# Eight token tiles turned in 32x32 blocks on VectorE and through DRAM, in place of TensorE transposes

## The chip, the cores and the metric

The kernel runs on one core of a Trainium2 chip. The metric is the time of one execution in device microseconds (us). The runs shown of the kernel before are 1119.29, 1119.57 and 1120.29 us; their median is 1119.57.

## The reference

The computation is one transformer-like block on x of 2048 tokens and 576 channels, in float32, where two branches work on the same normalised tokens:

```
xn  = (x - mean(x)) / sqrt(var(x) + 1e-5)            # over the 576 channels of each token
A   = attention(xn @ wqkv) @ wo                      # 32 heads of 18; each token looks at 8 keys,
                                                     # its own and those 2, 4, ... 14 tokens back
B   = mish(xn @ w1 + b1) @ w2                        # 576 -> 4608 -> 576
out = x + A + B
```

## The kernel before

The tokens are worked through in two halves of 1024 (`hf` 0 and 1), each half in two blocks of 512 tokens (`b`), each block in four tiles of 128 tokens (`jj`). A half runs through four stages: its tiles are normalised and transposed, the q, k and v products are made in groups of heads (`qkv_item`, L327), the feed-forward branch runs in 18 steps of `m1_part` (first product, Mish) and `m2_pair` or `m2_cols` (second product), and beside the feed-forward steps GpSimd and VectorE work on the attention. The output projection of both halves comes last.

A float32 operand is split into a high part, rounded to the type that TensorE multiplies, and a low part, the rest; three products (high x high, high x low, low x high) make one. So every tile of tokens has to be turned, with channels as rows, and split: `transpose_split` (L67) does it. TensorE turns four 128x128 pieces into one PSUM bank (L75), the last 64 channels into a second bank (L76), and for the second block the rests `rem` of the tile of the first block as well (L78). ScalarE rounds both banks into the high part in SBUF (L81, L86), VectorE subtracts that from the banks for the low part (L82, L87). Ahead of it ScalarE normalises the tile in place (`norm1`, L139) and GpSimd copies its last 64 channels once more beside them (L140), so that high and low of these channels share one matmul; GpSimd also keeps or subtracts `rem` (L192, L194).

The order of the work is written out by hand. A list `plan` holds the items of TensorE in order: `q` for a q, k and v product, `m` and `p` for the parts of a feed-forward step, `t` for a tile that is turned, `z` and `o` for others. `before(i, fn)` hangs other work onto item i: loads, casts, normalisation. When the program is built, the list is walked once and every engine gets its instructions in that order and keeps it. All DMAs are issued from SyncE's one queue (SP), in that order too; a DMA that waits holds up those behind it. The DMAs use eight semaphores in turn, so a DMA also waits until the one eight before it has landed.

Tiles in SBUF and PSUM come from pools with a fixed number of buffers per tag, used in turn; a new tile waits until the last user of the one before in its buffer is done. Those that matter here: `xn` (5 buffers: tokens and scratch), `raw` (4 buffers: weights as loaded), and in PSUM `h` and `out` (4 banks each). The matmuls of `m2_pair` (L759) write into `out` banks, which VectorE adds to the accumulators (L763), and the turned pieces of the second half's first three tiles take two `out` banks each. The matmuls of `m1_part` (L661, L667) and of `qkv_item` (L348) write into `h` banks; the Mish of a step reads one of them (L707), and an add on VectorE (L706) precedes the Mish of others.

The change lies where the first half ends and the second begins. The eight tiles of the second half are loaded (`x_load`, L103), normalised and turned (`tr`, L1222) while TensorE does the last three feed-forward steps of the first half and, for the second block, the first q, k and v products of the second half. The items around it are, in order: the step q = 17 with the second products of step 16 between its parts, and three turned tiles between those; the fourth turned tile; the second products of step 17, with q items of the second half between them; and a turned tile ahead of or behind each of the next q items.

Of the kernel before, what the change touches and what calls it, by code (L numbers as in the profile page):

```python
# [8 lines left out]
F32 = mybir.dt.float32  # L9
# [5 lines left out]
S, D, F = 2048, 576, 4608  # L15
H, DH, W, DIL = 32, 18, 8, 2
HALO = (W - 1) * DIL
P = 128
# [4 lines left out]
TJ = SH // P  # L23
JB = TJ // NB
KT = D // P
NF = F // P
NP = NF // 2
# [12 lines left out]
def block_kernel(ctx: ExitStack, tc: tile.TileContext, x, wq, wo, w1, b1, w2, mask, out):  # L40
    nc = tc.nc
    tpn = iter(range(1000))

    const = ctx.enter_context(tc.tile_pool(name="const", bufs=1))
    sb = ctx.enter_context(tc.tile_pool(name="sb", bufs=2))
    ps = ctx.enter_context(tc.tile_pool(name="ps", bufs=4, space=bass.MemoryType.PSUM))
    dram = ctx.enter_context(tc.tile_pool(name="dram", bufs=1, space=bass.MemoryType.DRAM))
# [13 lines left out]
    ident = const.tile([P, P], F32, name="ident")  # L61
# [2 lines left out]
    for k in range(30):  # L64
        nc.tensor.transpose(warm[:, (k % 4) * P:(k % 4 + 1) * P], ident, ident)

    def transpose_split(src, dst, col, extra=None, pair=False):  # L67
        n = next(tpn)
        if pair:
            ta, tb = (ps.tile([P, 512], F32, tag="out", bufs=4, name=f"tt{k}_{n}") for k in range(2))  # L70
        else:
            ta = ps.tile([P, 512], F32, tag="h", bufs=4, name=f"ta_{n}")
            tb = ps.tile([P, 512], F32, tag="h", bufs=4, name=f"tb_{n}")
        for k in range(KT):
            nc.tensor.transpose(ta[:, k * P:(k + 1) * P], src[:, k * P:(k + 1) * P], ident)  # L75
        nc.tensor.transpose(tb[:, 0:P], src[:, KT * P:(KT + 1) * P], ident)  # L76
        if extra is not None:
            nc.tensor.transpose(tb[:, P:2 * P], extra, ident)  # L78
        tav = ta.rearrange("p (k t) -> p k t", k=KT)
        hi = dst[:, 0:KT, col:col + P]  # L80
        nc.scalar.copy(hi, tav)  # L81
        nc.vector.tensor_sub(dst[:, 5:5 + KT, col:col + P], tav, hi.bitcast(F32))  # L82
        e = 1 if extra is None else 2
        hr = dst[:, KT:KT + 5 * e - 4:5, col:col + P]
        tbv = tb.rearrange("p (k t) -> p k t", k=KT)[:, 0:e]
        nc.scalar.copy(hr, tbv)  # L86
        nc.vector.tensor_sub(hr[64:P], tbv[64:P], hr[64:P].bitcast(F32))  # L87

    XTs = {}
    rems = {}  # L90
    xns = {}
    XNB = 5
# [7 lines left out]
    def x_tile(hf, n):  # L100
        return x[hf * SH:(hf + 1) * SH, :].rearrange("(p j) d -> p j d", j=TJ)[:, n, :]

    def x_load(n):  # L103
        xn = sb.tile([P, 5 * P], F32, tag="xn", bufs=XNB, name=f"xn_1_{n}_{next(tpn)}")
        nc.sync.dma_start(xn[:, 0:D], x_tile(1, n))
        xns[1, n] = xn

# [29 lines left out]
    def norm1(n):  # L137
        xn = xns[1, n]
        nc.scalar.activation(xn[:, 0:D], xn[:, 0:D], AF.Identity, bias=nm1[:, n, :], scale=rs1[:, n, :])  # L139
        nc.gpsimd.tensor_copy(xn[:, D:D + 64], xn[:, KT * P:D])  # L140

    group = {}

    def ln_group(ns):
# [39 lines left out]
    def ln_transpose(hf, b, jj):  # L184
        if jj == 0:
            XTs[hf, b] = sb.tile([P, 9 + b, TB], F32R, tag=f"xt{b}", bufs=1, name=f"xt_{hf}_{b}")
        xn = xns[hf, b * JB + jj]
        if (b, jj) == (0, 0):
            rems[hf] = sb.tile([P, JB, P], F32, tag="tt", bufs=2, name=f"rem_{hf}")
        rem = rems[hf][:, jj, :]  # L190
        if b == 0:
            nc.gpsimd.tensor_copy(rem, xn[:, KT * P:])  # L192
        else:
            nc.gpsimd.tensor_tensor(out=rem, in0=rem, in1=xn[:, KT * P:], op=ALU.subtract)  # L194
        transpose_split(xn, XTs[hf, b], jj * P, rem if b else None, (hf, b) == (1, 0) and jj < 3)

    def raw_load(src, width, name):
        raw = sb.tile([P, 5 * P], F32, tag="raw", bufs=4, name=f"r{name}")
# [176 lines left out]
    BUFS = {"wb": 3, "wc": 2, "wa0": 1, "a0": 3, "a1": 2, "acc": 9, "raw": 4, "tt": 2, "r3": 1, "mn": 5, "xn": XNB}  # L375
# [764 lines left out]
    at = {}  # L1140
# [7 lines left out]
    def before(i, fn):  # L1148
        plan[max(i, 0)][1].append(fn)
# [188 lines left out]
    def spot(hf, q, i):  # L1338
        return at["s", hf, q, i]

    for q in range(NP):
        if q == 0:
            i = at["q", 0, 3, 1, 0]
            ps_ = dict(raw=i - 3, sums=i - 1, wa=i, wc=i + 1, t0=i + 2, t1=i + 4)
        elif q == 1:
            i = at["q", 0, 3, 0, 0]
# [16 lines left out]
    for q in range(1, 2 * OC + 1):  # L1363
        i = spot(0, q, (3,2)[q > 1])
# [5 lines left out]
    i = spot(0, NP - 1, 0)  # L1370
# [5 lines left out]
    i = at["q", 1, 0, 1, 1]  # L1376
# [4 lines left out]
    i = spot(0, 9, 4)  # L1381
    for k in range(2):
        for n, steps in enumerate((
# [33 lines left out]
    for n, (a, b) in enumerate((("P6", "P1"), ("P7", "P6"), ("P6", "P5"), ("P2", "P1"), ("P3", "P6"), ("P4", "P7"), ("P5", "P7"))):  # L1417
        for pr in range(2):
            i = items[-2][2] + 1 + (0,1,2)[n] if n < 3 else at["p", 1, J + 0 - 1, n > 4, pr] + (1, 7, 1, 2)[n - 3]
# [6 lines left out]
    i = at["q", 0, 1, 1, 0]  # L1426
# [3 lines left out]
    i = at["q", 0, 3, 1, 0]  # L1430
# [5 lines left out]
    i = at["q", 1, 0, 1, 1]  # L1436
    for n in range(8):
        c, k = divmod(n, 4)
        d = i + (0, 1, 3, 4, 6, 8, 10, 12)[n]
        before(d, lambda c=c, k=k: s_step(1, c, k))  # L1440
        d = max(d + 2, (at["q", 1, 1, 1, 2], at[("z", 1, 2)])[c] if k == 3 else 0)
# [4 lines left out]
    for n in range(0, JB, 2):  # L1446
        i = at["q", 0, 1, 0, n]
# [4 lines left out]
    for n in range(TJ):  # L1452
        i = spot(0, 2 + n, 2)
        before(i, lambda n=n: x_load(n))
        before(i + 5, lambda n=n: stats1(n))
    before(i + 6, var1)
    i = spot(0, NP - 2, 0)
    for jj in range(JB):
        before(i + 2 * jj, lambda jj=jj: x_load(jj))
        before(i + 2 * jj + 6, lambda jj=jj: norm1(jj))  # L1460
        before(at["t", 1, 0, jj] + 2, lambda jj=jj: x_load(JB + jj))
    for jj in range(JB):
        before(at["p", 0, NP - 1, 1, 1] + jj, lambda jj=jj: norm1(JB + jj))

    for n, (name, pr) in enumerate((name, pr) for name in ("P4", "P5", "P2", "P3") for pr in range(2)):
        i = items[dict(P4=0, P5=2, P3=2, P2=3)[name]][2] + pr
# [122 lines left out]
```

## Time and profile before

| what | value |
|---|---|
| median of the runs | 1119.57 us |
| span of the profiled execution | 1118.2 us |
| what lies around the span, by that median | 1.4 us |
| TensorE busy | 1109.2 us, 99% |
| VectorE busy | 835.2 us, 75% |
| GpSimd busy | 777.4 us, 70% |
| ScalarE busy | 491.7 us, 44% |
| time taken by DMA packets, share of 16 engines | 69.8% on SP's queue |
| granted clock of TensorE | 1.00 |

The profiled execution has no time of its own beside its span; the time that lies around it is taken as the difference to the median of the runs. In the profile PE is TensorE, PEld its weight loads, DVE is VectorE, ACT ScalarE, POOL GpSimd and SPq the queue of SyncE from which the DMAs are issued. A line such as `L75` is a line of the kernel before. A row of the timeline gives the start in us, the duration, the engine, the line, the operation with output and inputs, the count, and in brackets how long the engine sat idle before it and what released it. A row of the DMA issues gives output and input, the count, the size of each and the median time from issue to landing.

### The profile page before, as it was taken

The numbers are of one execution on the slowest core, as the hardware profiler recorded it, in microseconds if no ns is written. First come the engines' busy times: TensorE is split into PE (matmuls) and PEld (weight loads), VectorE is DVE, ScalarE is ACT, GpSimd is POOL, SyncE is SP. The second block draws the span as 40 slices with busy tenths as digits, with TensorE's granted clock in tenths as the row PEclk, the third lists the DMA queues.
The fourth block names the chain that finished last, engine by engine and source line by source line (L and its number), as shares of the span: only waits on it lengthen the run. The fifth ranks groups of instructions, "written<-read, shape, count | busy, mean of one in ns | idle before, by whom it ended". The sixth has DMA issues, their size and how long they took to land.

```text
span 1118.2 us, 18402 instructions
## 1 busy us (share of the span) xinstructions
PE 1109.2 (99%) x6630; PEld 1023.9 (92%) x6630; DVE 835.2 (75%) x1355; ACT 491.7 (44%) x892; POOL 777.4 (70%) x631
## 2 busy tenths in 40 slices
PE   8999999999999999999999999999999999999998
PEld 8999899999999999999999888989999999999998
DVE  6369788888888888887656566687866677776876
ACT  5544645544554545555233354343433343443332
POOL 2479777767689687685787346666789878668632
PEclk9999999999999999999999999999999999999999
DMA  6899695868767849666696797665655477576463
GB/s 200 284 311 313 227 357 205 294 227 282 260 241 265 273 169 342 226 240 215 208 332 234 240 378 254 225 200 188 220 192 190 173 266 270 207 258 243 160 217 108
DMA packets 147487, 271.08 MB, mean 242 GB/s; under 512 B 30114, under 2 KB 86724, under 8 KB 147396
## 3 DMA queue, kind: packets, MB, share of 16 engines
q1 hardware_dynamic: 147396, 269.91, 69.8%
q8 instruction: 52, 0.85, 0.3%
q14 instruction: 39, 0.32, 0.1%
HBM read 160.39 MB, written 109.48 MB: 241 GB/s over the span
## 4 chain that ended last, share of the span: by engine, by line
PE 94%; DVE 3%; POOL 1%; ACT 1%; issue 1%; DMA 0%; SPq 0%; DVEq 0%; POOLq 0%; ACTq 0%
PE h L661 30%; PE po L759 20%; PE pq L348 11%; PE po L872 10%; PE po L851 7%; PE h L667 6%; PE o L1060 4%; PE z L446 4%; POOL accP L860 1%; DVE accP L875 0%; POOL act L713 0%; DMA acc<-in_x 0%; PE ta L75 0%; DVE og L582 0%; POOL act L814 0%
## 5 line engine op out<-in xcount | busy, mean ns | idle before, releaser
L759 PEld LDWEIGHTS po<-w,act 128*128 128x128 f32 x1728 | 236.4, 188 | 6.0 <-POOL act L713 0.4
L759 PE MATMUL po<-w,act 128*128 128x288 f32 x1728 | 240.7, 295 | 0.1
L576 POOL TENSOR_TENSOR pv<-L,kv 128x576 f32<-128x576 f32 x128 | 176.3, 1477 | 38.5 <-DVE L L569 28.9
L713 POOL TENSOR_TENSOR act<-c,act 128x512 fp32r<-128x512 f32 x81 | 107.6, 1329 | 126.1 <-ACT act L712 124.4
L538 POOL TENSOR_TENSOR pr<-q,kv 128x576 f32<-128x576 f32 x120 | 184.2, 1564 | 7.7 <-DMA q<-q_d 6.0
L763 DVE TENSOR_TENSOR acc<-po,acc 128x288 f32<-128x288 f32 x288 | 120.0, 449 | 31.8 <-PE po L759 30.5
L348 PE MATMUL pq<-wq,xt 128*128 128x432 f32 x672 | 136.4, 361 | 1.2 <-ACT xt L81 1.2
L872 PEld LDWEIGHTS po<-w,act 128*128 128x128 f32 x960 | 131.1, 188 | 3.7 <-DVE accP L875 0.4
L872 PE MATMUL po<-w,act 128*128 128x288 f32 x960 | 133.8, 295 | 0.2
L348 PEld LDWEIGHTS pq<-wq,xt 128*128 128x128 f32 x672 | 125.0, 188 | 8.2 <-ACT xt L81 2.1
L707 ACT ACTIVATE c<-c,b1c 128x512 f32<-128x512 f32 x81 | 58.7, 725 | 130.6 <-DVE c L706 130.2
L661 PE MATMUL h<-S,t 128*128 128x512 f32 x432 | 110.4, 391 | 0.0
L661 PE MATMUL h<-xt,t 128*128 128x512 f32 x432 | 110.4, 391 | 0.0
L695 ACT COPY c<-h 128x512 f32<-128x512 f32 x81 | 47.5, 586 | 133.2 <-PE h L667 75.2
L582 DVE TENSOR_REDUCE og<-pv 128x144 f32<-128x1152 f32 x64 | 85.9, 1343 | 26.8 <-POOL pv L576 26.7
L661 PE MATMUL h<-xt,wa 128*128 128x512 f32 x432 | 104.1, 390 | 0.0
L543 DVE TENSOR_REDUCE L<-pr 128x64 f32<-128x1152 f32 x64 | 85.8, 1342 | 17.6 <-POOL pr L538 17.4
L875 DVE TENSOR_TENSOR accP<-po,accP 128x288 f32<-128x288 f32 x160 | 69.7, 454 | 38.9 <-PE po L872 37.4
L661 PEld LDWEIGHTS h<-xt,wa 128*128 128x128 f32 x432 | 80.9, 188 | 17.0
L851 PEld LDWEIGHTS po<-pw,u 128*128 128x128 f32 x672 | 92.2, 188 | 2.9 <-DVE u L805 0.7
L851 PE MATMUL po<-pw,u 128*128 128x288 f32 x672 | 93.7, 295 | 0.4 <-DVE u L805 0.4
L661 PEld LDWEIGHTS h<-xt,t 128*128 128x128 f32 x432 | 79.1, 188 | 14.7 <-DVE rt L706 0.2
(232 smaller groups left out, 1848.7 us busy)
## 6 DMA issues: line engine op xcount, KB each, us to landing
kv<-kv_d SPq DMA_DIRECT2D x64, 396.0 KB, 5.6
kept_t<-t SPq DMA_DIRECT2D x36, 512.0 KB, 5.2
t<-kept_t SPq DMA_DIRECT2D x36, 512.0 KB, 5.0
rw<-in_w SPq DMA_DIRECT2D x36, 320.0 KB, 4.5
kept_wa<-wa SPq DMA_DIRECT2D x18, 640.0 KB, 4.7
kept_w<-w SPq DMA_DIRECT2D x20, 576.0 KB, 4.1
wa<-kept_wa SPq DMA_DIRECT2D x18, 640.0 KB, 6.3
w<-kept_w SPq DMA_DIRECT2D x20, 576.0 KB, 4.7
```

What stands on the lines that cost most here:

```text
L348: nc.tensor.matmul(pq[:, 0:432], XT[:, xi, tok], wt[wi][:, hl, 0:432], start=i == 0, stop=i == len(seq) - 1)
L538: nc.gpsimd.tensor_tensor(out=pr[:, x:x + hh], in0=q[:, j0 + x:j0 + x + hh, None, :].to_broadcast([P, hh, W, CU]), in1=win(kt, 0, CU, j0 + ...
L543: nc.vector.tensor_reduce(L[:, k, j0:j0 + hj].rearrange("p j w h -> p (j w h)"), pr.rearrange("p j w (h d) -> p (j w h) d", h=2), axis=AX, ...
L576: nc.gpsimd.tensor_tensor(out=pr[:, x:x + hj].rearrange("p j d w -> p j w d"), in0=L[:, k, x:x + hj, :, h:h + 1].to_broadcast([P, hj, W, DH]),
L582: nc.vector.tensor_reduce(og[:, :, c0:c0 + DH], pr, axis=AX, op=ALU.add)
L661: nc.tensor.matmul(ph, wt[:, wl, wk * P:(wk + 1) * P], X[:, xs, :], start=first and i == 0, stop=last and i == len(seq) - 1, skip_group_ch ...
L713: nc.gpsimd.tensor_tensor(out=a[:, 1, :], in0=t, in1=a[:, 0, :].bitcast(F32), op=ALU.subtract)
L759: nc.tensor.matmul(po, acts[hf, q, b, j][:, al, tok], done["w2", hf, 2 * q + j][:, wl, c * HC:(c + 1) * HC], start=i == 0, stop=i == 5)
L763: nc.vector.tensor_tensor(out=t, in0=po, in1=t, op=ALU.add)
L851: nc.tensor.matmul(po, units[e, k, qq][:, al, tok], w[:, qq, wl, :], start=i == 0, stop=i == 5)
L872: nc.tensor.matmul(po, acts[hf, q, b, j][:, al, tok], done["w2", hf, 2 * q + j][:, wl, c * HC:(c + 1) * HC], start=i == 0, stop=i == 5)
L875: nc.vector.tensor_tensor(out=t, in0=po, in1=t, op=ALU.add)
```

## The change

TensorE no longer turns the eight tiles of the second half. Instead:

- VectorE transposes a tile's 32x32 blocks (`x_turn`): within each block of 32 tokens and 32 channels rows and columns change places. The result goes into one SBUF buffer (tag `oT`, one buffer).
- Four DMAs write it, 32 partitions each, to a DRAM tensor of 576 channels by 128 tokens; each moves 576 pieces of 32 elements (128 bytes). Three DMAs read it back (`x_back`) into an `xn` buffer with channels as rows: 512 channels as four pieces side by side, and the last 64 twice, one below the other.
- `transpose_split` copies the read tile with ScalarE into the PSUM banks where TensorE put its result, and the split goes on as before. The second block's `rem` is copied in the same way.
- GpSimd's copy of the last 64 channels in `norm1` is gone, as the double read takes its place.
- Loads, normalisation, turning and reading back have new places in the list. The loads of the second block go to `raw` buffers.

In the order of each engine the change gives the following. TensorE has 44 transposes fewer and is otherwise in the same order. On VectorE the block transposes of the first block stand in step 16: the first behind the first four accumulates (L763) of the second products of step 15, the others behind the later groups of four (the second with one subtraction between). Those of the second block stand behind the split of the second tile, behind the next four accumulates, behind the split of the third tile, and behind the first four accumulates of step 17. On SP, the last tiles' writes and reads stand among the loads of `kv`, `q` and `wq`, some of which come behind them.

```
-    def transpose_split(src, dst, col, extra=None, pair=False):
+    def transpose_split(src, dst, col, extra=None, pair=False, turned=False):
         n = next(tpn)
+        turn = (lambda o, i: nc.scalar.copy(o, i)) if turned else (lambda o, i: nc.tensor.transpose(o, i, ident))
...
-        for k in range(KT):
-            nc.tensor.transpose(ta[:, k * P:(k + 1) * P], src[:, k * P:(k + 1) * P], ident)
-        nc.tensor.transpose(tb[:, 0:P], src[:, KT * P:(KT + 1) * P], ident)
+        if turned:
+            turn(ta, src[:, 0:KT * P])
+        else:
+            for k in range(KT):
+                turn(ta[:, k * P:(k + 1) * P], src[:, k * P:(k + 1) * P])
+        turn(tb[:, 0:P], src[:, KT * P:(KT + 1) * P])
         if extra is not None:
-            nc.tensor.transpose(tb[:, P:2 * P], extra, ident)
+            turn(tb[:, P:2 * P], extra)
...
-        nc.gpsimd.tensor_copy(xn[:, D:D + 64], xn[:, KT * P:D])
-
+
+    def x_turn(n):
+        t = sb.tile([P, D], F32, tag="oT", bufs=1, name=f"xT_{n}")
+        nc.vector.transpose(t, xns[1, n][:, 0:D])
+        d = xT_d[n] = dram.tile([D, P], F32, name=f"xT_d{n}")
+        rows = d.rearrange("(n i) p -> i n p", i=32)
+        for g in range(4):
+            part = slice(g * 32, (g + 1) * 32)
+            nc.sync.dma_start(rows[:, :, part], t[part].rearrange("i (n k) -> i n k", k=32))
+
+    def x_back(n):
+        xn = xns[1, n] = sb.tile([P, 5 * P], F32, tag="xn", bufs=XNB, name=f"xn_t_{n}")
+        nc.sync.dma_start(xn[:, 0:KT * P].rearrange("p (k t) -> p k t", k=KT),
+                          xT_d[n][0:KT * P].rearrange("(k p) t -> p k t", p=P))
+        for r_ in range(2):
+            nc.sync.dma_start(xn[r_ * 64:(r_ + 1) * 64, KT * P:], xT_d[n][KT * P:D])
...
-    i = spot(0, NP - 2, 0)
-    for jj in range(JB):
-        before(i + 2 * jj, lambda jj=jj: x_load(jj))
-        before(i + 2 * jj + 6, lambda jj=jj: norm1(jj))
-        before(at["t", 1, 0, jj] + 2, lambda jj=jj: x_load(JB + jj))
-    for jj in range(JB):
-        before(at["p", 0, NP - 1, 1, 1] + jj, lambda jj=jj: norm1(JB + jj))
+    i, e = spot(0, NP - 3, 8), at["t", 1, 0, JB - 1]
+    for n in range(TJ):
+        b_, jj = divmod(n, JB)
+        turn = e - 4 + 2 * jj if b_ else i + 2 * jj + 5
+        load_at = spot(0, NP - 1, 0) + (1, 2, 4, 6)[jj] if b_ else i + 2 * jj
+        back = e + (1, 2, 4, 7)[jj] if b_ else turn + 4
+        before(load_at, lambda n=n: x_load(n, "raw" if n >= JB else "xn"))
+        before(turn - 1, lambda n=n: norm1(n))
+        before(turn, lambda n=n: x_turn(n))
+        before(back, lambda n=n: x_back(n))
```

More of the change, by code (lines that the diff above doesn't have):

```diff
@@ L101, in x_tile, with x_load @@
         return x[hf * SH:(hf + 1) * SH, :].rearrange("(p j) d -> p j d", j=TJ)[:, n, :]
-    def x_load(n):
-        xn = sb.tile([P, 5 * P], F32, tag="xn", bufs=XNB, name=f"xn_1_{n}_{next(tpn)}")
+    def x_load(n, tag="xn"):
+        xn = sb.tile([P, 5 * P], F32, tag=tag, bufs=BUFS[tag], name=f"xn_1_{n}_{next(tpn)}")
         nc.sync.dma_start(xn[:, 0:D], x_tile(1, n))
@@ L139, in norm1 @@
         nc.scalar.activation(xn[:, 0:D], xn[:, 0:D], AF.Identity, bias=nm1[:, n, :], scale=rs1[:, n, :])
-        nc.gpsimd.tensor_copy(xn[:, D:D + 64], xn[:, KT * P:D])
+    def x_turn(n):
[12 more added lines that the diff above has]
+            nc.sync.dma_start(xn[r_ * 64:(r_ + 1) * 64, KT * P:], xT_d[n][KT * P:D])
+    xT_d = {}
     group = {}
@@ L194, in ln_transpose @@
             nc.gpsimd.tensor_tensor(out=rem, in0=rem, in1=xn[:, KT * P:], op=ALU.subtract)
-        transpose_split(xn, XTs[hf, b], jj * P, rem if b else None, (hf, b) == (1, 0) and jj < 3)
+        transpose_split(xn, XTs[hf, b], jj * P, rem if b else None, (hf, b) == (1, 0) and jj < 3, hf == 1)
     def raw_load(src, width, name):
```

## The prediction

> **What bounds the kernel now.** I read the page's busy times and its chain first, then the chain in order of time, then the timeline of each engine where the second half's tokens are turned (485 to 560 us), then the DMA shares there.
>
> ```profile
> PE 1109.2 (99%) x6630; PEld 1023.9 (92%) x6630; DVE 835.2 (75%) x1355; ACT 491.7 (44%) x892; POOL 777.4 (70%) x631
> ...
> PE 94%; DVE 3%; POOL 1%; ACT 1%; issue 1%; DMA 0%; SPq 0%; DVEq 0%; POOLq 0%; ACTq 0%
> ```
>
> TensorE is busy for 99% of the span and carries 94% of the chain. So a TensorE instruction taken away is worth its whole time, and any microsecond in which TensorE is made to wait is lost whole; nothing later can absorb it.
>
> **What is removed.** The chain in order of time, columns start, us, what:
>
> ```profile
> 513.52 0.44 PE tt L75 x4
> 513.96 0.11 PE tt L76
> 514.07 1.39 PE h L661 x6
> ...
> 545.87 0.44 PE ta L75 x4
> 546.31 0.11 PE tb L76
> 546.42 0.11 PE tb L78
> 546.53 2.77 PE pq L348 x14
> ```
>
> The eight tiles of the second half lose 44 TensorE transposes. A tile of the first block costs 0.55 us (513.52 to 514.07), one of the second 0.66 us (545.87 to 546.53), and there are four of each: 4 x 0.55 + 4 x 0.66 = 4.84 us, all on the path. This is the whole gain. The eight 64-column copies on GpSimd go too; GpSimd is at 70% and not on the path here, so they are worth nothing.
>
> **What is added, by price.** A row of the page's costliest groups; two of ScalarE's timeline; three DMA issues; the source view of the og store; two lines of the DMA view of 482 to 483 us:
>
> ```profile
> L543 DVE TENSOR_REDUCE L<-pr 128x64 f32<-128x1152 f32 x64 | 85.8, 1342 | 17.6 <-POOL pr L538 17.4
> ```
>
> ```profile
> 514.00 0.59 ACT L81 CAST xt<-tt 128x512 fp32r<-128x512 f32 x1 [0.68 <-PE tt L75]
> 514.48 0.27 ACT L86 CAST xt<-tt 128x128 fp32r<-128x128 f32 x1
> ```
>
> ```profile
> o_d<-og SPq DMA_DIRECT2D x16, 288.0 KB, 3.4
> ...
> y_d<-acc SPq DMA_DIRECT2D x8, 288.0 KB, 2.1
> ...
> out<-accP SPq DMA_DIRECT2D x16, 144.0 KB, 1.8
> ```
>
> ```profile
> L584 SPq DMA_DIRECT2D o_d<-og x16: 513/519/755, 142.4 to 1057.8; - x16
> ```
>
> ```profile
> DMA packets 802, 0.23 MB, mean 231 GB/s; under 512 B 802, under 2 KB 802, under 8 KB 802
> ...
> q1 hardware_dynamic: 802, 0.23, 98.9%
> ```
>
> VectorE: eight block transposes of 128x576, which this trace has nowhere. The reduce streams 1152 columns in 1.34 us, so 576 columns are 0.67 us; at twice that rate 0.35, at half 1.34. I take 0.7.
> ScalarE: a 512-column and a 128-column copy per tile, a second 128-column one in the second block: 0.59 + 0.27, or 0.59 + 2 x 0.27, together 8.0 us over 60 us in which ScalarE is under half busy. I cost it at nothing: TensorE's work hides it. Without that cover it would cost up to 1.1 us a tile. The loads and norms of all tiles move up, four loads into raw buffers; none of them is late for its transpose, so they cost nothing.
> DMA: per tile four writes of 576 packets of 128 B and three reads of 640 packets of 512 B, 56 more DMAs on SP's queue. From 482 to 483 us the 288 B packets of one og store ran: 16 x 0.989 us / 802 = 19.7 ns a packet. A 128 B packet costs between its share of the bytes, 8.9 ns, and the full 19.7 ns: 1.3 to 2.8 us of all 16 engines per tile, and I take 2.0.
> The trip: call L the time from the first write's issue to the last one's landing. Issues take 0.32 to 0.52 us, I take 0.45, so the fourth starts 1.35 us after the first. The og store lands in 3.4 us with 1.3 us of packets (802 took 1 us); a part has 0.3 to 0.7 us of them, so some 2.4 us in a quiet queue: L = 1.35 + 2.4 = 3.75. Ends: 3 x 0.32 + 1.8 = 2.8, and 3 x 0.45 + 3.4 = 4.75.
>
> **The new wait.** The turned tile has one buffer (tag oT). So each VectorE transpose waits until the previous tile's four writes have landed, and VectorE waits in program order, with all behind it. In VectorE's order the places of the transposes, on the clock of before, are about 485.4, 492.1, 494.9, 499.9, then 521.9, 525.1, 527.3, 531.5. A round needs 0.7 + L + 0.1 = 4.5 us. Three gaps are shorter: 2.8 (second to third tile), 3.2 and 2.2 (fifth to sixth to seventh).
>
> **First wait (third tile).** VectorE, ScalarE and TensorE there, then the DMA shares (last two columns of a window: DMA share, GB/s):
>
> ```profile
> 490.41 1.71 DVE L255 TENSOR_TENSOR wc<-rw,wc 128x384 fp32r<-128x384 f32 x1
> ...
> 494.86 1.34 DVE L543 TENSOR_REDUCE L<-pr 128x64 f32<-128x1152 f32 x1
> 496.12 1.33 DVE L255 TENSOR_TENSOR t<-tt,t 128x512 fp32r<-128x512 f32 x1
> 497.36 0.68 DVE L706 TENSOR_TENSOR c<-h,c 128x512 f32<-128x512 f32 x1
> ```
>
> ```profile
> 498.08 0.72 ACT L707 ACTIVATE c<-c,b1c 128x512 f32<-128x512 f32 x1 [2.65 <-DVE c L706]
> ...
> 499.36 1.25 ACT L254 CAST w<-rw 128x576 fp32r<-128x576 f32 x2
> ...
> 501.31 0.69 ACT L707 ACTIVATE mn<-h,b1c 128x512 f32<-128x512 f32 x1
> ```
>
> ```profile
> 501.11 2.88 PE L661 MATMUL h<-xt,wa 128*128 128x512 f32 x12
> ```
>
> ```profile
> 485.00:490.00 5.00, 5.00 (x34) 4.67 (x33) 4.39 (x6) 1.00 (x2) 5.00 (x4) 1.00 1.04 419
> 490.00:495.00 5.00, 5.00 (x34) 4.68 (x33) 4.43 (x9) 3.56 (x6) 2.73 (x4) 1.00 1.02 406
> 495.00:500.00 5.00, 5.00 (x34) 4.68 (x33) 4.66 (x8) 2.32 (x5) 4.38 (x5) 1.00 0.93 369
> ```
>
> Read it as a relay. VectorE's add (497.36) releases ScalarE's Mish (498.08), its cast and two weight casts, and behind them stands the Mish of 501.31, which frees the PSUM bank that TensorE's second six matmuls of the item at 501.11 need, at 501.11 + 1.36 = 502.5. From the third transpose's start to that bank: 0.7 + 1.26 + 1.25 + 0.65 on VectorE, then 0.75 + 0.5 + 1.15 + 0.7 on ScalarE (the norm that stood here has moved ahead), 7.0 us. In line it would start at 495.4 (494.9, and 0.5 for its two predecessors), giving 502.4. There is no slack left: each microsecond that it waits is a microsecond of TensorE.
> The second transpose ends near 492.9. In a quiet queue its writes land at 496.7, 1.3 us of wait. But the queue is full from 485 to 500 (shares 0.93 to 1.04). In SP's order o_d, kv, kept_t, xn, kept_w, the first tile's writes, kv, kept_w, rw, xn, kept_wa and rw stand ahead of the second tile's writes. At about 410 GB/s (288 KB 0.72, 512 KB 1.3, 576 KB 1.4, 640 KB 1.6, 396 KB 1.0, with og 1.3 and the tile 2.0) they are 13.8 us of DMA from 482.2 on, so these writes run from 496.0 to 498.0 and land at about 499.1. Wait 499.1 - 495.4 = 3.7 us, ends 0.35 (L 2.8, quiet) and 5.5 (packets at 19.7 ns). I take 3.7, since the shares show the queue full.
>
> **Second wait (sixth and seventh tile).** VectorE, then TensorE:
>
> ```profile
> 525.08 1.34 DVE L582 TENSOR_REDUCE og<-pv 128x144 f32<-128x1152 f32 x1
> 526.34 0.68 DVE L82 TENSOR_TENSOR xt<-tt,xt 128x512 fp32r<-128x512 f32 x1
> ...
> 528.96 0.69 DVE L82 TENSOR_TENSOR xt<-ta,xt 128x512 fp32r<-128x512 f32 x1 [1.62 <-ACT xt L81]
> ...
> 530.01 1.55 DVE L763 TENSOR_TENSOR acc<-po,acc 128x288 f32<-128x288 f32 x4
> ```
>
> ```profile
> 527.37 2.89 PE L759 MATMUL po<-w,act 128*128 128x288 f32 x20
> 529.83 4.15 PE L759 MATMUL po<-w,act 128*128 128x288 f32 x30
> ```
>
> TensorE would reach the second group of 24 po matmuls at 530.55 + 3.7 - 4 x 0.55 = 532.05. Its first PSUM bank (four of them) comes free with the first accumulate of the 530.01 row, which in the new order stands behind the sixth and seventh transposes. The fifth starts near 525.3 (same shifts, behind ScalarE's copies). Sixth: 526.05 + 3.75 = 529.8. Seventh: 530.55 + 3.75 = 534.3. Then 0.7, the two subtractions of the fourth tile 0.95, the accumulate 0.45: bank free at 536.4. TensorE waits 4.3 us (2L - 3.2; ends 2.4 at L 2.8 and 6.3 at L 4.75). SP's kv, q and wq loads, moved behind these writes, land 0.7 us before their matmuls at this pace and cost nothing more; if TensorE did not wait for VectorE, the fifth wq tile, behind the seventh tile's writes, would be late instead by about 2 us. The read back of each tile has 9 us or more to spare; a tile that came late would stop ScalarE in order.
>
> **Sum.** -4.84 + 3.7 + 4.3 = +3.2 us on the profiled span of 1118.2, so 1121.4; the median of the runs, 1119.57, lies 1.4 above that span, so **1122.7 us** (+0.3%). Ends: -4.84 + 0.35 + 2.4 = -2.1 (1117.5) and -4.84 + 5.5 + 6.3 = +7.0 (1126.6).
>
> **Two rules against the change.** The Trainium skill, page "DMA: Bandwidth & Descriptors", Specifications, puts line rate at 512 B and more and says that below it the DMA does read-modify-write. The trace agrees in direction: 231 GB/s at 288 B against 419 GB/s in the full window. Page "TensorE: Matmul & The Clock Gate", Part 1, says that an idle window of about 3.4 us halves the clock; no row here shows it, the granted clock is 1.00 in every window and TensorE never rests that long.
>
> **Rivals.**
> - *The waits are hidden; only the gain is left.* If writes land before VectorE comes to the next transpose, or the two banks are not the ones that bind: 1119.57 - 4.84 = 1114.7. For it: VectorE has idle time (75% busy). Against: the 2.2 us gap is less than even L = 2.8. It turns at waits of 2.6 us together, below which the gain passes 0.2%. Chance 0.15.
> - *Small waits, break-even.* Quiet queue for the second tile (1.3) and L of 3.0 (2.8): -0.7, 1118.8. Chance 0.2.
> - *Small packets are dear.* At twice 19.7 ns a tile's writes are 5.7 us of DMA; two tiles add 7.4 us to the full queue ahead of the third transpose, and L grows by 1.1: 3.7 + 7.4 + 6.5 - 4.84 = +12.8, 1132.3. It is what the first rule would do here. Against: og lands in 3.4 us. Chance 0.07.
> - *The clock falls.* Two waits of about 4 us; if after each some 3 us of matmuls ran at half rate, each adds 1.5 to 3 us: 1125.7 to 1128.7. It is what the second rule would do. Chance 0.08.
> - The forecast, waits of 5 to 12 us together: chance 0.5.
>
> **How the numbers follow.** 0.2% (2.24 us) is about what a measurement of this kernel can tell from no change. Faster: the first rival, 0.15. Same: break-even and a little of the forecast's lower end, 0.26. Slower: the rest of the forecast and both slow rivals, 0.59. The range leaves out half of the first rival and the dear packets: 1116 to 1128.5. Forecast alone: 1119.8 to 1126.6.
>
> **What will show it.** 44 fewer TensorE matmuls, busy time about 5 us less. VectorE idle before the block transposes, released by a DMA write of xT_d, some 4 us before the third, 2 to 4 before the sixth and seventh. TensorE idle near 502 (released by ScalarE's Mish, L727 there) and between 530 and 537 (by accumulates). Block transposes of 0.6 to 0.8 us. Wrong if VectorE doesn't wait there, if TensorE's idle time is under 5 us or elsewhere (a late wq or read back), or if the granted clock leaves 1.00.

## Result and profile after: slower by 0.7%

The changed kernel takes 1127.39 us (median of four runs, 1126.46 to 1128.26) against 1119.57 before: 1.0069 times as long, 95% interval 1.0057 to 1.0081. The forecast was 1122.7 in a range from 1116 to 1128.5: the sign was right, the size was 4.7 us short. The profiled execution of the changed kernel has a span of 1126.5 us, 8.3 more than the one before; its own time was 1128.26, 0.9 us above the median.

The page of the changed kernel, busy times and chain:

```profile
PE 1109.4 (98%) x6586; PEld 1022.2 (91%) x6586; DVE 837.5 (74%) x1363; ACT 497.8 (44%) x912; POOL 776.1 (69%) x623
...
PE 88%; DVE 5%; DMA 2%; ACT 2%; POOL 1%; issue 1%; SPq 1%; DVEq 0%; ACTq 0%; POOLq 0%
```

TensorE's 44 transposes are gone (6630 instructions are 6586), but its busy time is the same; 3.5 of the 4.84 us are two rows of matmuls below that ran at half clock. VectorE, DMA, ScalarE and SP's queue have taken 6 points of the chain from TensorE. Who waited between 480 and 570 us (us in total, times, longest):

```profile
DVE xT L147 <- DMA xT_d<-xT: 14.5, 4, 7.0
...
PE po L779 <- DVE xt L86: 3.3, 1, 3.3
PE po L779 <- DVE w L275: 1.5, 1, 1.5
PE po L779 <- POOL act L733: 1.3, 2, 0.8
PE po L779 <- DVE acc L783: 0.9, 1, 0.9
```

The block transposes (L147) waited four times for the writes of the tile before them. On VectorE's timeline:

```profile
501.26 0.78 DVE L147 STREAM_TRANSPOSE xT<-xn 128x576 f32<-128x576 f32 x1 [6.96 <-DMA xT_d<-xT]
...
531.70 0.78 DVE L147 STREAM_TRANSPOSE xT<-xn 128x576 f32<-128x576 f32 x1 [3.65 <-DMA xT_d<-xT]
...
536.13 0.78 DVE L147 STREAM_TRANSPOSE xT<-xn 128x576 f32<-128x576 f32 x1 [1.50 <-DMA xT_d<-xT]
...
541.91 0.78 DVE L147 STREAM_TRANSPOSE xT<-xn 128x576 f32<-128x576 f32 x1 [2.38 <-DMA xT_d<-xT]
```

They are the third, sixth, seventh and eighth tile; the block transpose itself takes 0.77 to 0.78 us, and the second tile's had begun at 491.44. What this did to TensorE is read by setting its timelines side by side, the same items before and after. Before (the item at 501.11 stands in the prediction):

```profile
508.82 1.53 PE L661 MATMUL h<-S,t 128*128 128x512 f32 x6
...
527.37 6.61 PE L759 MATMUL po<-w,act 128*128 128x288 f32 x48
533.82 2.92 PE L348 MATMUL pq<-wq,xt 128*128 128x432 f32 x14
...
586.94 2.52 PE L446 MATMUL z<-zacc_B,xt 128*128 128x432 f32 x12
```

After:

```profile
500.47 2.88 PE L681 MATMUL h<-xt,wa 128*128 128x512 f32 x12
...
504.62 1.63 PE L681 MATMUL h<-xt,t 128*128 128x512 f32 x6 [0.81 <-DVE c L726]
...
507.30 0.53 PE L779 MATMUL po<-w,act 128*128 128x288 f32 x2 [0.79 <-POOL act L733]
509.29 2.93 PE L779 MATMUL po<-w,act 128*128 128x288 f32 x20 [1.46 <-DVE w L275]
512.05 1.53 PE L681 MATMUL h<-S,t 128*128 128x512 f32 x6
...
528.50 0.42 PE L779 MATMUL po<-w,act 128*128 128x288 f32 x2
...
534.36 3.25 PE L779 MATMUL po<-w,act 128*128 128x288 f32 x12 [3.34 <-DVE xt L86]
538.50 5.37 PE L779 MATMUL po<-w,act 128*128 128x288 f32 x24 [0.89 <-DVE acc L783]
543.71 2.92 PE L368 MATMUL pq<-wq,xt 128*128 128x432 f32 x14
...
561.94 4.28 PE L368 MATMUL pq<-wq,xt 128*128 128x432 f32 x20 [0.65 <-DVE xt L91]
...
595.18 2.52 PE L466 MATMUL z<-zacc_B,xt 128*128 128x432 f32 x12
```

The distance between the kernels goes -0.64 us (501.11 to 500.47, there before the change begins), +3.23 (508.82 to 512.05), +1.13 (527.37 to 528.50), +9.89 (533.82 to 543.71), +8.24 (586.94 to 595.18). So the first wait cost TensorE 3.87 us, the first block's transposes gave 2.10 back, the second group of waits cost 8.76, and the second block gave back 1.65. The granted clock fell inside the second group (columns as in the prediction; the third number from the end is the clock, and it was 0.50 from 534 to 542 us):

```profile
534.00:536.00 2.00, 1.64 (x7) 1.64 (x8) 0.60 (x2) 0.00 (x0) 2.00 (x2) 0.50 0.95 130
```

Last, SP's issues of the writes (the eight from 525.89 on are those of the fifth and the sixth tile), and from the DMA view of 534 to 535 us the packets and the share of the 16 engines that they took:

```profile
492.23 4.23 SPq L152 DMA_DIRECT2D xT_d<-xT  x4
...
525.89 8.57 SPq L152 DMA_DIRECT2D xT_d<-xT  x8
...
536.93 2.10 SPq L152 DMA_DIRECT2D xT_d<-xT  x4
```

```profile
DMA packets 1077, 0.14 MB, mean 135 GB/s; under 512 B 1077, under 2 KB 1077, under 8 KB 1077
...
q1 hardware_dynamic: 1077, 0.14, 87.3%
```

From a tile's first issue to the moment when its buffer is free (the start of the next block transpose) it is 9.0 us for the second tile (492.23 to 501.26), 5.8 for the fifth (525.89 to 531.70), 3.6 for the sixth (its writes begin at 532.50), 5.0 for the seventh (536.93 to 541.91). A packet of 128 B takes 16 x 0.873 us / 1077 = 13.0 ns.

### The profile page after: what moved, and what is told of

The parts are those of the page before. It is cut to its first block, busy times and chain, and to the rows that moved or that the text cites. A ratio compares the mean times of both kernels' runs of the same rounds, so it can differ in the third digit from the quotient of the medians.

```text
span 1126.5 us, 18409 instructions
## 1 busy us (share of the span) xinstructions
PE 1109.4 (98%) x6586; PEld 1022.2 (91%) x6586; DVE 837.5 (74%) x1363; ACT 497.8 (44%) x912; POOL 776.1 (69%) x623
## 4 chain that ended last, share of the span: by engine, by line
PE 88%; DVE 5%; DMA 2%; ACT 2%; POOL 1%; issue 1%; SPq 1%; DVEq 0%; ACTq 0%; POOLq 0%
PE h L681 27%; PE po L779 19%; PE pq L368 11%; PE po L892 10%; PE po L871 6%; PE h L687 5%; PE o L1080 4%; PE z L466 3%; DMA xT_d<-xT 1%; SPq L152 1%; DMA xn<-in_x 1%; POOL accP L880 1%; DVE L L563 0%; DVE accP L895 0%; POOL act L733 0%
## 5 line engine op out<-in xcount | busy, mean ns | idle before, releaser
L779 PE MATMUL po<-w,act 128*128 128x288 f32 x1728 | 245.3, 298 | 7.1 <-DVE xt L86 3.3
L892 PE MATMUL po<-w,act 128*128 128x288 f32 x960 | 133.8, 295 | 0.2
```

The source lines that it names most:

```text
L779: nc.tensor.matmul(po, acts[hf, q, b, j][:, al, tok], done["w2", hf, 2 * q + j][:, wl, c * HC:(c + 1) * HC], start=i == 0, stop=i == 5)
L892: nc.tensor.matmul(po, acts[hf, q, b, j][:, al, tok], done["w2", hf, 2 * q + j][:, wl, c * HC:(c + 1) * HC], start=i == 0, stop=i == 5)
```

## The experiments

The theory after the result: the one buffer is what costs, through the time L that a tile's writes take; the halved clock adds some 3.5 us on top (12 matmuls of 3.25 us and 24 of 5.37, at full clock about 1.75 and 3.35). Rivals: the DMA traffic costs, wherever the buffers are; the gain itself is smaller than counted; the clock costs nothing.

| kernel | median, us | ratio to before, 95% interval |
|---|---|---|
| changed kernel | 1127.39 | 1.0069 [1.0057, 1.0081] |
| e1, three buffers | 1124.46 | 1.0038 [1.0025, 1.0051] |
| e2, no transposing at all | 1117.89 | 0.9984 [0.9975, 0.9993] |
| e3, first block alone | 1122.87 | 1.0030 [1.0020, 1.0040] |
| e4, second block alone | 1122.41 | 1.0025 [1.0015, 1.0034] |
| e5, writes in wide rows | 1123.35 | 1.0035 [1.0023, 1.0046] |
| e6, TensorE kept busy, one place | 1128.12 | 1.0070 [1.0055, 1.0085] |
| e7, second block turned late | 1125.20 | 1.0047 [1.0032, 1.0062] |
| e8, e7 and late splits | 1120.73 | 1.0009 [0.9999, 1.0018] |
| e9, e6 again | 1128.06 | 1.0073 [1.0059, 1.0087] |
| e10, first block alone, three buffers | 1118.63 | 0.9989 [0.9981, 0.9998] |
| e11, e10 and late splits | 1116.69 | 0.9971 [0.9959, 0.9982] |
| e12, TensorE kept busy, three places | 1128.61 | 1.0074 [1.0060, 1.0088] |

The kernel before had medians of 1119.61 to 1119.85 us beside them.

**e1: three buffers.**

```
-        t = sb.tile([P, D], F32, tag="oT", bufs=1, name=f"xT_{n}")
+        if n % 3 not in turns:
+            tag, width, bufs = (("oT", D, 1), ("acc", D, 9), ("r3", 2 * 432, 1))[n % 3]
+            turns[n % 3] = sb.tile([P, width], F32, tag=tag, bufs=bufs, name=f"xT_{n}")
+        t = turns[n % 3][:, 0:D]
```

> The block transposes of the tiles write in turn into three buffers in place of one (two of the three lie idle at this point of the kernel: the ninth of tag acc and the one of tag r3). Theory (the one buffer is the cause: VectorE waits for the landing of the tile before, TensorE waits behind VectorE): the waits of the transposes, 14.5 us in the changed kernel, fall below 1 us, TensorE's idle time there with them, and the gain of the removed transposes shows: 1114.5 to 1117 us. Rival (the cost is the traffic itself: 56 more DMAs with 128 B packets in a full queue make loads and casts late): still 1121 us or more.

1124.46 us: 2.9 us of the 7.8 lost are back. That is the rival's number and not the theory's, though no block transpose waits any more, as the theory had it. TensorE's timeline of e1 shows what is late next:

```profile
530.74 3.46 PE L782 MATMUL po<-w,act 128*128 128x288 f32 x24 [1.57 <-DVE acc L786]
...
536.01 1.46 PE L371 MATMUL pq<-wq,xt 128*128 128x432 f32 x6 [0.62 <-DMA wq<-kept_wq]
539.36 0.66 PE L371 MATMUL pq<-wq,xt 128*128 128x432 f32 x2 [1.90 <-DMA wq<-kept_wq]
```

The `wq` loads stand behind the writes on SP, as the prediction said they would if TensorE did not wait for VectorE (it said about 2 us; 2.5 in all). The wait for the accumulates (L786) was not foreseen. Behind these waits the granted clock was 0.5 for 3.4 us from 540.6 us on: the 24 matmuls after the `wq` waits took 4.87 us and not 3.35.

**e2: no block transposes, no writes, no reads.** ScalarE copies the unturned tile in their place.

```
-        before(turn, lambda n=n: x_turn(n))
-        before(back, lambda n=n: x_back(n))
```

> The block transposes, the writes to DRAM and the reads back are left out (part of the computation is left out: ScalarE copies the tile to PSUM unturned); GpSimd copies the last 64 channels as before the change. It shows what the removed TensorE transposes are worth if ScalarE's copies hide. Forecast of the prediction: 4.84 us, so 1114.7 us. Rival (ScalarE's copies, 8.0 us in all, come on the path): 1117 us or more.

1117.89 us, a gain of 1.7 us, where TensorE has lost 4.84 us of work. Who waited in e2 from 480 to 575 us:

```profile
PE po L780 <- DVE acc L784: 1.5, 1, 1.5
PE pq L369 <- DVE xt L91: 0.6, 1, 0.6
```

So even a trip that cost nothing would have gained a third of what was counted. VectorE and ScalarE ahead of the 1.5 us wait:

```profile
528.39 0.69 DVE L86 TENSOR_TENSOR xt<-ta,xt 128x512 fp32r<-128x512 f32 x1 [2.30 <-ACT xt L85]
```

```profile
527.07 0.58 ACT L69 COPY ta<-xn 128x512 f32<-128x512 f32 x1
...
527.78 0.58 ACT L85 CAST xt<-ta 128x512 fp32r<-128x512 f32 x1
```

TensorE's transposes had covered this path. The subtractions of the third and fourth tile stand ahead of the accumulates in VectorE's order, and the fourth tile's wait 2.30 us for ScalarE. ScalarE shows no idle time there from 522.41 us on; ahead of the fourth tile's high part stand the copies of the third and the fourth tile, 0.7 us a tile, and a norm of the second block. In the kernel before, the first accumulate of the 530.01 row freed its bank at 530.46, 0.1 us before TensorE needed it; with TensorE 2.3 us earlier in e2 (525.10 against 527.37), it comes 1.5 us late. The 0.6 us wait also ends at a split that waits for ScalarE (2.04 us), which copies that tile of the second block from 548.57 to 549.66. So the number is that of the rival, 1117 us or more: ScalarE's copies lie on both paths, though their share of the 1.5 us was not tested alone. In e10, where the norms of the second block stand behind the fourth tile, that wait is 1.0 us.

**e3 and e4: the first or the second block alone.** The other block is transposed by TensorE. In both, the rest of the last 64 channels of the second block is made from one tile with channels as rows and one with tokens as rows, so that part of the computation is changed; the work is the same.

```
-        before(turn, lambda n=n: x_turn(n))
-        before(back, lambda n=n: x_back(n))
+        if n < JB:                     # e4: n >= JB
+            before(turn, lambda n=n: x_turn(n))
+            before(back, lambda n=n: x_back(n))
```

> Only the four tiles of the first block go through DRAM; the second block's are turned on TensorE as before the change, at the changed places of load and norm. Theory: gain 2.2 us, loss from the third tile's wait 3.9 us, granted clock 1.00: 1121.3 us. Rival (the first block costs as much as its 7 us wait): 1124 us.

> Only the four tiles of the second block go through DRAM; the first block's are turned on TensorE. Theory: gain 2.6 us, loss near 530 to 543 us 8.8 us with a granted clock of 0.5 there, and 0.6 near 562: 1126 us. Rival (the second block's wait is a follow of the first block's lateness): 1119 us or less, granted clock 1.00.

+3.3 and +2.8 us against 1119.61. e3 lies between its theory (1121.3) and its rival (1124), e4 between its rival (1119) and its theory (1126), so neither theory's number was met. Each half of the change loses alone. In e3 VectorE waits 6.3 us before the third transpose, in e4 5.5 us in three waits, the longest 2.2:

```profile
532.87 3.46 PE L781 MATMUL po<-w,act 128*128 128x288 f32 x24 [1.52 <-DVE acc L785]
```

```profile
533.55 3.46 PE L781 MATMUL po<-w,act 128*128 128x288 f32 x24 [2.77 <-DVE acc L785]
```

(TensorE in e3, then in e4.) Together they are 6.1 of the 7.8 us of the whole change. Why the whole is more than its halves was not tested; e3 shows that the first block's splits alone make VectorE's accumulates late by 1.5 us (the fourth tile's waits 2.31 us for ScalarE, as in e2), and the second block's transposes stand among these accumulates.

The granted clock is 1.00 in both profiled executions, but not in every run. In e3 five runs at 1.00 took 1121.78 to 1122.87 us and four at 0.998 took 1123.53 to 1124.02; in e4 three at 1.00 took 1121.27 to 1121.89 and seven at 0.997 or 0.998 took 1122.17 to 1124.03. By the medians the runs in which the clock fell were 1.7 and 0.9 us longer. Whether the fallen clock made them longer, or a longer wait brought both, is not shown.

**e5: the same bytes in wide rows.**

```
-        rows = d.rearrange("(n i) p -> i n p", i=32)
+        rows = d.rearrange("c p -> (c p)").rearrange("(q d) -> q d", d=D)
...
-            nc.sync.dma_start(rows[:, :, part], t[part].rearrange("i (n k) -> i n k", k=32))
+            nc.sync.dma_start(rows[part], t[part])
```

> The writes carry the same bytes from the same partitions, in rows of 2304 bytes, not in pieces of 128 bytes. The DRAM tensor then does not hold channels as rows, so this kernel computes other numbers; the time of every step is meant to stand. Theory A, the 128-byte pieces fill the DMA engines (a tile's writes took 13 ns a packet, 2304 packets over 16 engines, 1.9 us; in wide rows about 0.7): the 7.0 us wait of VectorE before the third transpose falls to about 4, and the total of 1127.4 us to 1121.5 to 1124.5. Rival B, the size of the pieces does not matter, only the landing and the full queue: wait about 7, total 1126 to 1128.

1123.35 us: written in wide rows the change loses 4.0 us less of the 7.8, as theory A had it in the total. The first wait fell less than it said, from 7.0 to 5.3:

```profile
499.83 0.78 DVE L147 STREAM_TRANSPOSE xT<-xn 128x576 f32<-128x576 f32 x1 [5.26 <-DMA xT_d<-xT]
```

In wide rows too the second tile's writes landed 5.2 us after their issue (median of the four; 5.4 in the changed kernel). Loads and stores of weights stand ahead of them in SP's order; that these are what is left of the wait was not tested.

**e6 and e9: TensorE kept busy in its longest wait.** e9 was meant to hold 12 more transposes, but they were not in the kernel that ran; it is e6 a second time.

```
+            if (hf, q, b, jj) == (0, NP - 1, 1, 1):
+                fill = ps.tile([P, 512], F32, tag="h", bufs=4, name="fill")
+                for k in range(24):
+                    nc.tensor.transpose(fill[:, (k % 4) * P:(k % 4 + 1) * P], ident, ident)
```

> 24 extra transposes of the identity on TensorE, about 2.6 us, go between the first ten and the next matmuls of the second products of step 17, where TensorE idled 3.3 us; they write a bank that nobody reads. Theory A, the idle time halves the clock and this costs 3.5 us: granted clock 1.00 throughout, total 1123.2 to 1124.8 though more work is done. Rival B, the clock is lost for another reason, or costs nothing since TensorE waits there anyway: total 1126.5 to 1130.

> As e6, where the extra transposes kept the clock up at 534 us but it was halved at 511 to 514 us instead, behind a stretch with two short waits. 12 more transposes of the identity, about 1.4 us, go ahead of the first second product of step 16, in that stretch, into the columns of its own bank that the product then overwrites. Theory A, the clock is halved for 3.4 us whenever TensorE was busy for less than half of the 3.4 us before: no such stretch is left, granted clock 1.00, total 1124 to 1126 (1127.4 less 1.5 to 3.5). Rival B, what the clock takes is TensorE's waiting time anyway: total 1127 or more.

1128.12 and 1128.06 us: no gain. But the clock had only moved: in e6 it was now halved at another place, behind the two short waits of step 16.

```profile
509.76 4.37 PE L783 MATMUL po<-w,act 128*128 128x288 f32 x20 [1.45 <-DVE w L275]
```

```profile
512.00:514.00 2.00, 2.00 (x10) 2.00 (x10) 1.30 (x4) 1.35 (x2) 1.05 (x2) 0.50 0.88 254
```

(The timeline of TensorE and a window of e6; those 20 matmuls take 2.93 us in the changed kernel.) So neither theory was decided.

**e12: kept busy in all three places.**

```
+            if (hf, q, b, jj) in ((0, NP - 1, 1, 1), (0, NP - 1, 1, 2)):
+                if jj == 1:
+                    fill.append(ps.tile([P, 512], F32, tag="h", bufs=4, name="fill"))
+                for k in range(24 if jj == 1 else 16):
+                    nc.tensor.transpose(fill[0][:, (k % 4) * P:(k % 4 + 1) * P], ident, ident)
...
+                for k in range(12 if (hf, q, b, jj, c) == (0, NP - 2, 1, 0, 0) else 0):
+                    nc.tensor.transpose(po[:, (k % 2) * P:(k % 2 + 1) * P], ident, ident)
```

> The kernel of e9 was the one of e6 once more: its 12 further transposes were not in it, and the clock was halved from 508 to 512 us and from 540 to 543 us again. Here they are in: 12 transposes of the identity (1.4 us) ahead of the first second product of step 16, 24 (2.8 us) inside the wait near 531 us as in e6, and 16 (1.9 us) inside the wait near 537 us. They lie in TensorE's waiting time, and no 3.4 us are left in which it is busy for less than half. Theory A, the halved clock costs 1.5 us each time it falls on work: granted clock 1.00, total 1124 to 1126 (the changed kernel has 1127.4, with one to three such stretches). Rival B, what the clock takes is TensorE's waiting time anyway: 1127 or more.

The granted clock is 1.00 in all five runs, and the time is 1128.61 us (1126.18 to 1129.63): no gain, rival B. TensorE in e12:

```profile
538.70 3.46 PE L788 MATMUL po<-w,act 128*128 128x288 f32 x24 [0.64 <-DVE acc L792]
541.99 2.92 PE L368 MATMUL pq<-wq,xt 128*128 128x432 f32 x14
545.32 3.45 PE L788 MATMUL po<-w,act 128*128 128x288 f32 x24 [0.40 <-DVE acc L792]
```

The 24 matmuls start when VectorE frees their bank, at 538.70 as at 538.50 in the changed kernel. At full clock they take 1.9 us less, and then TensorE waits for the next accumulates, behind the eighth tile's transpose. At the first `z` item e12 is 1.05 us ahead of the changed kernel (594.13 against 595.18; it was 0.78 behind at the item of 500.47), and 0.98 us of waiting for VectorE follows in the `z` items, which the changed kernel does not have. So most of what the clock gave was lost again to VectorE, and the time is the same as far as these runs can tell: by the two intervals a gain of more than some 1.5 us is excluded (an estimate), and with it the 3.5 us of the theory.

**e7: the second block turned behind the `wq` loads.** With e1's buffers:

```
-        turn = e - 4 + 2 * jj if b_ else i + 2 * jj + 5
+        turn = e + 2 + jj if b_ else i + 2 * jj + 5
...
-        back = e + (1, 2, 4, 7)[jj] if b_ else turn + 4
+        back = e + 5 + jj if b_ else turn + 4
```

> As e1 (three buffers), and the last four tiles are turned later, behind the wq loads, and read back later. Theory A, what was left in e1 was the wait for wq loads behind the writes (2.5 us) and the slow clock behind it (1.5 us): no wait for wq, clock 1.00, total 1118 to 1120, near the kernel without any turning (1117.9). Rival B, the traffic of the turned tiles itself delays the loads wherever it stands: total 1122 or more.

1125.20 us, as slow as e1: theory A was wrong, and the number is rival B's. There is no wait for `wq`, but the tiles come back late. SP, ScalarE and TensorE in e7:

```profile
536.09 5.82 SPq L155 DMA_DIRECT2D xT_d<-xT  x8
...
542.98 0.45 SPq L159 DMA_DIRECT2D xn_t<-xT_d  x1
```

```profile
546.41 0.59 ACT L69 COPY ta<-xn_t 128x512 f32<-128x512 f32 x1 [3.91 <-DMA xn_t<-xT_d]
```

```profile
549.36 3.04 PE L371 MATMUL pq<-wq,xt 128*128 128x432 f32 x14 [1.53 <-DVE xt L91]
...
559.20 7.11 PE L371 MATMUL pq<-wq,xt 128*128 128x432 f32 x27 [2.48 <-DVE xt L91]
```

The writes of the sixth and seventh tile hold SP's queue until 542 us, so the fifth tile is read back from 543 us on, and its copy waits until 546.41; the three later tiles follow in the same way (TensorE waits 5.3 us for their splits, with a stretch at half clock from 560 us on). Turned early, the second block's writes delay the loads behind them; turned late, its reads are late. Neither of the two places was free.

**e8: e7 with the third and fourth tile split behind the accumulates.**

```
-            if (hf, q) == (0, NP - 1) and i in (5, 7, 9):
+            if (hf, q) == (0, NP - 1) and i in (5, 7):
...
-            tr(0, 3)
...
+                if jj < 2:
+                    tr(0, 2 + jj)
```

> As e7, and the third and fourth tile are split behind the accumulates of the second products of step 17, not ahead of them. Theory A, the 1.5 us wait of TensorE for the accumulates, which was left in the kernel without any turning, goes as well: total 1116 to 1118, faster than before. Rival B, the splits come late for the q items that read them, or the accumulates were not what bound: total 1118.5 or more.

1120.73 us, 4.5 less than e7 and about the time of the kernel before: neither theory's number, but A's direction. Of TensorE's wait for the accumulates, 1.0 us in e7, 0.3 is left; the waits for xt fall from 5.3 to 3.2 us, and waits for `wq` come back (1.2). At the first `z` item 1.0 us of the gain is there; behind it e7 waits another 1.0 us for VectorE in the `z` items and 0.5 for VectorE at 751 us, and e8 does not. These are 2.5 of the 3.2 us between the two profiled executions (that of e8, 1122.30, is its slowest of ten). What is left of the 4.5 was not traced.

**e10 and e11: only the first block turned, with three buffers; in e11 with e8's late splits.** TensorE turns the second block; VectorE makes its rest in the PSUM bank. Both compute the whole of the reference.

```
+        if mixed:
+            nc.vector.tensor_sub(tb[:, P:2 * P], extra, tb[:, 0:P])
-        if extra is not None:
+        elif extra is not None:
             turn(tb[:, P:2 * P], extra)
...
+        if n < JB:
+            before(turn, lambda n=n: x_turn(n))
+            before(back, lambda n=n: x_back(n))
```

> Only the first block is turned on VectorE and through DRAM, into three buffers as in e1; TensorE turns the second block as before. The rest of the last 64 channels of the second block is subtracted on VectorE from the PSUM bank, so the whole computation stands. Theory A: no wait for the one buffer; 20 TensorE transposes (2.2 us) and 4 more (0.4 us) go, and the 1.5 us wait of TensorE for the accumulates, behind VectorE's splits, is left: 1119.6 - 2.6 + 1.5 = 1118.5, range 1117.8 to 1119.3, clock 1.00. Rival B, the traffic of four tiles alone already delays loads: 1120 or more.

> As e10, and the third and fourth tile are split behind the accumulates of the second products of step 17, as in e8. Theory A, the 1.5 us wait for the accumulates goes too: 1116.5 to 1117.5, faster than before. Rival B, the later splits come late for the q items that read them (PE waits for xt), and eat the gain: 1118 to 1120.

1118.63 and 1116.69 us, both as theory A had them. e11 is 0.29% faster than the kernel before (interval 0.18 to 0.41%) and 0.95% faster than the changed kernel. TensorE in e11, where the 48 matmuls of the two chunks run without a wait, 2.3 us earlier than before (527.37 to 525.09):

```profile
525.09 6.53 PE L786 MATMUL po<-w,act 128*128 128x288 f32 x48
531.45 3.11 PE L375 MATMUL pq<-wq,xt 128*128 128x432 f32 x14
```

At the first `z` item e11 is 2.3 us ahead (584.66 against 586.94); the other 0.9 us of its span come later, 0.4 of it from the wait for VectorE at 746 us, which is gone here as in e8. The rest was not traced. e8 turns the second block as well and takes 4.0 us more than e11: with three buffers and late splits that is what the second block's trip costs, over and above its own gain.

## Why the prediction was right, and where it was not

- *What bounds.* "A TensorE instruction taken away is worth its whole time" was wrong. Of the 4.84 us e2 kept 1.7, since VectorE's accumulates stood 1.5 us behind TensorE and a split of the second block another 0.6. The trace of before could have shown it: the bank that TensorE needed at 530.55 came free at 530.46, so it could not have moved ahead without waiting. e11, with the splits moved, gets the gain of its 24 transposes (4 x 0.55 + 4 x 0.11 = 2.64 us) and a little more.
- *ScalarE's copies.* "I cost it at nothing: TensorE's work hides it" was wrong in e2, where both waits end at ScalarE, though it is busy for less than half of the span: in that stretch it had no idle time. It held in e11, where the splits of the third and fourth tile stand behind the accumulates.
- *Prices.* The block transpose was taken at 0.7 us and takes 0.77. A tile's packets were taken at 2.0 us of 16 engines; at 13.0 ns they are 2304 x 13.0 / 16 = 1.87. The time that lies around the span was taken as 1.4 us, by the median; every run that has both shows 1.7 to 1.9, so the profiled execution of before was a run of about 1119.95 and the forecast's sum, with 1.75 in its place, 1123.1. On the packets the Trainium skill, page "DMA: Bandwidth & Descriptors", Specifications, has line rate only from 512 B on and read-modify-write below. The trace agrees that they are slow, at 135 GB/s with 128 B and 231 GB/s with 288 B; whether read-modify-write is the reason no run shows. e5 puts the price of the small pieces at 4.0 us.
- *L.* This is the term that was mis-sized. 3.75 us was worked out for a quiet queue; measured are 9.0, 5.8, 3.6 and 5.0. Only the sixth tile met it, whose writes found a quiet queue (DMA shares of 0.10 and 0.27 from 530 to 534 us). The upper end, 4.75, was no bound either.
- *First wait.* The mechanism and the tile were right, the wait was 7.0 and not 3.7 (the writes landed at 501.26 and not 499.1, and VectorE came at 494.30 and not 495.4), and "there is no slack left" was wrong: TensorE lost 3.87. That this is close to 3.7 is luck; the two errors cancelled. The bank that the relay was to end in did not bind: the twelve matmuls at 500.47 ran through. What TensorE waited for was VectorE's add (0.81), GpSimd's low part (0.79) and VectorE's subtraction for the weights (1.46), each behind the late transpose in VectorE's order.
- *Second wait.* The place was right (VectorE 3.65 and 1.50 us before the sixth and seventh tile, and 2.38 before the eighth, which was not foreseen); 4.3 us became 8.76. TensorE waited first for a split (L86), which the prediction had not named, and then for the accumulates. This is the term that missed most. The trips of the fifth and sixth tile took 9.4 us and not 7.5, and the last 24 matmuls took 2.0 us more at half clock; how the 8.76 divides further was not traced.
- *The clock.* The rival that gave it 0.08 was right that it falls, which the prediction itself had named as a sign of being wrong, and the measured 1127.39 lies in its interval (1125.7 to 1128.7), above the forecast's own upper end of 1126.6. But e12, at 1.00 throughout, is no faster, so in the changed kernel the clock did not add 1.5 to 3 us at each wait. My own 3.5 us after the result was wrong for the same reason. In e3 and e4 the runs in which the clock fell are longer, and there the question stays open.
- *The other rivals.* Waits that are hidden (1114.7) and small waits (1118.8) are out with 14.5 us of waiting. Dear packets (1132.3) are out by 13.0 ns. The late `wq` tile was rightly named as next in line (e1). "The read back of each tile has 9 us or more to spare": no engine's wait for a read back shows in the changed kernel between 480 and 570 us, and in e7 it does.

In the changed kernel's trace the terms of the sum come out as 3.87 for the first wait (forecast 3.7), 8.76 for the second (4.3) and a gain of 2.10 + 1.65 = 3.75 (4.84). The total lies above the forecast because the second wait was sized with a quiet queue and without the split and the clock, and because the gain was counted whole; it stayed within the stated range with the help of the luck in the first wait.

## What to carry to other kernels

An engine that is busy for 99% still covers work of others: before its instructions are counted as gain, look how far ahead it can move until another engine's order stops it (e2 kept 1.7 of 4.84 us), and look for idle time of the engine that takes over the work in that very stretch and not in the average of the span. A buffer that is written out by DMA should be sized by the time to landing measured in the same stretch of the queue, not in a quiet one, and a trip through DRAM that costs nothing for four tiles (e11) can cost 4 us for the next four (e8 against e11), whose writes and reads stand among loads that TensorE needs next. A halved clock, or any slow stretch of an engine, need not be a cost: if another engine is late at its end, as in e12, nothing is gained by mending it, and yet in e3 the runs without it were 1.7 us shorter, from whichever cause. Keep the engine busy and look before the microseconds are booked.

## What the hardware showed beyond that

The granted clock fell without a long rest of TensorE. In e8 the longest gap was 1.81 us, and the clock was 0.5 for 3.4 us from 554 us on (0.49 / 0.5 x 2 us and 0.37 / 0.5 x 2 us in these two windows):

```profile
549.01 2.98 PE L371 MATMUL pq<-wq,xt 128*128 128x432 f32 x14 [1.42 <-DVE xt L91]
553.80 6.52 PE L371 MATMUL pq<-wq,xt 128*128 128x432 f32 x24 [1.81 <-DVE xt L91]
```

```profile
554.00:556.00 2.00, 2.00 (x7) 1.81 (x7) 1.06 (x2) 1.07 (x4) 2.00 (x2) 0.51 1.04 216
556.00:558.00 2.00, 2.00 (x8) 1.86 (x7) 1.41 (x2) 0.00 (x0) 2.00 (x4) 0.63 0.97 370
```

In the 3.4 us before, from 550.6 to 554.0, TensorE was busy for 1.35 + 0.25 = 1.6 us, 47%. The same working gives 45% in e1, 46% in e6 and 43% in e7, each followed by about 3.4 us at 0.5; the changed kernel, which waited on, stayed at 0.5 for 10 us. In the profiled execution of e5 two gaps of 1.84 and 1.83 us left the clock at 1.00, where five of its seven runs show 0.996 to 0.998, and e6 and e9, one kernel, lost it at different places. The Trainium skill, page "TensorE: Matmul & The Clock Gate", Part 1, states a free-running window of about 3.4 us and a fall after an idle one; the length agrees, and so do the shifting places, but here a window that was somewhat under half busy was enough, if the window that decides is the 3.4 us right before the fall, which is assumed. Where the limit lies above 47% was not tried.
